# Eight attention units at the front of a fused attention and MLP kernel: two units per 128 partitions, and the maximum subtracted by matrix product

## The chip, the core and the metric

The kernel runs on one core of a Trainium2 chip. The metric is the device time of one execution, in microseconds (us); the median of three runs before the change is 599.78 us (599.56 to 600.16).

The engines named here: TensorE (PE in the profile, PEld for its weight loads) does matrix products into PSUM, VectorE (DVE) and ScalarE (ACT) do elementwise work and read PSUM, GpSimd (POOL) works on SBUF only, SyncE (SP) issues the DMAs.

## The reference

Chunked attention with memory keys, then an MLP with a learned leak. All data are float32.

```python
batch, n_heads, seq, head_dim = 4, 8, 768, 64;  n_mem = 8
chunk, left_ctx, right_ctx = 32, 16, 8
for c in range(seq // chunk):            # 24 chunks of 32 queries
    k_ctx = k[:, :, max(0, 32*c - 16) : min(seq, 32*c + 40)]
    k_full, v_full = concat(mem_k, k_ctx), concat(mem_v, v_ctx)   # up to 64 keys
    scores = q_c @ k_full.T / 8
    a = exp(scores - max(scores));  a = a / (sum(a) + 1e-9)
    out[:, :, chunk c] = a @ v_full
x = out, heads side by side              # 3072 x 512
h = x @ w_in                             # 512 x 2048
g = max(h, 0) + alpha * min(h, 0)
return g @ w_out                         # 2048 x 512
```

## The kernel before, in words

**Units.** Attention is cut into 32 units: a half sequence of 384 tokens (BT) of one batch, times a pair of heads. Four units (NPAIR) make one block of x with 384 tokens and 512 features. Unit u fills feature slice k = u % 4 of half u // 4. The first eight units (NWIN) form blocks 0 and 1. They go another way than the later 24, and the change is about this way; it is written in `windows(u)`.

**One front unit**, step by step, all float32:

- `load_first(u)`: two DMAs into one of four buffers `early` (NSET): queries and keys (656 KB), then values (256 KB). In the queries the two heads stand block-diagonally, with zeros, so that one product serves both heads.
- `score_products(u)` (L300): two filler products (`stir`, L298; eight for unit 0), then 12 products with 128 rows (both heads), 64 output rows and 64 keys. Each float32 product is two instructions. The result is one PSUM bank, `s0` or `s1` by turns: 128 partitions by 6 windows of 64 keys.
- `top` (VectorE, L505 to L509): hides keys outside the sequence and takes the maximum of each window; `less` (VectorE, L513) subtracts it into SBUF; `exps` (ScalarE, L517); `total` and `inverse` (VectorE, L521 and L524).
- `scale` (GpSimd, L534 and L538, three instructions): multiplies with the inverse and writes into `ew`, where each 64-key window has its place in a zeroed field of 128.
- `turn` (L541): one filler product and six 128 x 128 transposes on TensorE, into banks `o0` and `o1`; `keep` (ScalarE, L551, twice) copies them to SBUF.
- `values` (L553): 8 products with 128 rows, 64 output rows and 96 columns, into bank `o2` or `a` by turns.
- `split` (L465): x is kept as a high part (`xh`, ScalarE, L474) and a low part (`xl`, VectorE, L477), both in the reduced float format that TensorE takes in one pass.

**The MLP.** For each block and each of 16 slices f of the hidden width, `up` (L723) makes 12 products of 384 columns (4 feature slices x 3 combinations of high and low parts), `below`, `bend`, `high` and `low` (L732 to L745) apply the leak and split the result, `down` (L753) makes 9 products of 512 columns. For f below 2 the four feature slices of `up` are steps of their own, so each can start when its own unit's x is there. Blocks 0 and 1 alternate for the first nine slices.

**Weights** are loaded as 64-bit integers' raw halves and rebuilt on the chip (`decode`, L609 to L650): ScalarE rebias (L622), a gather on VectorE or ScalarE (L630), VectorE `ends` (L634) and `join` (L638), ScalarE `high` (L646), VectorE `low` (L649). Two buffers `a` hold the work in progress. The weights 12 to 15 later take the place of the four `early` buffers.

**Order.** Nothing is left to a run-time scheduler. Every piece is a `step(engine, cost, function, reads, writes, rest)`. The planner (`Plan.send`) works out what remains behind each step, adds the entries of SHIFT by step number, and deals steps to each engine's queue, the longest remainder first, among those that its own costs and due times say are ready. Each engine, SP with its DMAs too, then runs its queue strictly in that order.

Of the kernel before, what the change touches and what calls it, by code (L numbers as in the profile page):

```python
# [102 lines left out]
STIR = (8, 2, 1)  # L103
# [4 lines left out]
NWIN, NSET = 2 * NPAIR, 4  # L108

STARTS_WIN = (0, 2 * LEFT, NKT - KW)  # L110
NQ = NT * NJ * 2 * CH
NV = NT * 2 * D

# [6 lines left out]
SHIFT = {3: -3.7, 9: -2.7, 10: 2.2, 11: 5.5, 44: 3.5, 63: -3.2, 65: -3.3, 96: -3.1, 103: -3.8, 112: 8.6, 114: 3.6, 116: -15.4, 174: 3.9}  # L120
# [61 lines left out]
def body(ctx: ExitStack, tc: tile.TileContext, qvw, kw, first, w_in, w_out, alpha, out):  # L182
# [17 lines left out]
    ps_a = ctx.enter_context(tc.tile_pool(name="ps_a", bufs=1, space=bass.MemoryType.PSUM))  # L200

# [19 lines left out]
    for ew in ews:  # L221
        nc.gpsimd.memset(ew, 0.0)
# [6 lines left out]
    state = {}  # L229
# [70 lines left out]
    def score_products(u):  # L300
        blk, pr = divmod(u, NPAIR)
        st = state[u]
        s_ps = ps_s.tile([P, 512], F32, name="s_ps", tag=f"s{u % 2}")
        stir(s_ps, STIR[0] if u == 0 else STIR[1])
        st["s"] = s_ps[:, :2 * NJ * KW].rearrange("p (n k) -> p n k", k=KW)
        t = early[u % NSET]
        q = t[:, :NQ].rearrange("p (c x) -> p c x", c=NT * NJ)
        keys = t[:, NQ:NQ + NT * NKT].rearrange("p (t k) -> p t k", t=NT)
        for n in range(2 * NJ):
            for i in range(2):  # L310
                t, j = n // NJ * 2 + i, n % NJ
                nc.tensor.matmul(  # L312
                    out=st["s"][i * 2 * CH:(i + 1) * 2 * CH, n],
                    lhsT=q[:, t * NJ + j],
                    rhs=keys[:, t, STARTS_WIN[j]:STARTS_WIN[j] + KW],
                    start=True, stop=True,
                )
# [114 lines left out]
    def value_products(u):  # L432
        st = state[u]
        pool, tag, _ = bank(u)
        st["a"] = pool.tile([P, 512], F32, name="a_ps", tag=tag)
# [29 lines left out]
    def split(u, ak="a"):  # L465
# [5 lines left out]
        cols = slice(at_ * BT, (at_ + 1) * BT)  # L471

        def high():
            nc.scalar.copy(out=ring[k][0][:, cols], in_=st["a"][:, :BT])  # L474

        def low():
            nc.vector.tensor_tensor(out=ring[k][1][:, cols], in0=st["a"][:, :BT], in1=ring[k][0][:, cols].bitcast(F32),  # L477
                                    op=ALU.subtract)
# [3 lines left out]
        step(ACT, 0.48, high, reads=[ak], writes=xh)  # L482
        step(DVE, 0.56, low, reads=[ak, xh[0]], writes=xl)

    def load_first(u):
        blk, pr = divmod(u, NPAIR)
        t = early[u % NSET]

        def load(lo, hi):
            nc.sync.dma_start(out=t[:, lo:hi], in_=first[blk, pr, :, lo:hi])  # L490

        state[u] = {}
        step(SP, 1.6, partial(load, 0, NQ + NT * NKT), writes=[("qk", u % NSET)], rest=due(u))
        step(SP, 0.78, partial(load, NQ + NT * NKT, NQ + NT * NKT + NV), writes=[("fv", u % NSET)], rest=due(u))

    def windows(u):

        st = state[u]
        sk, tks, ak = ("s", u % 2), [("o", 0), ("o", 1)], ("o", 2) if u % 2 else "a"
# [11 lines left out]
        def less():  # L511
            st["e"] = es[u % 2][:, :, :KW]
            nc.vector.tensor_tensor(out=st["e"], in0=st["s"], in1=st["mx"].broadcast_to([P, NJ * 2, KW]),  # L513
                                    op=ALU.subtract)

        def exps():
            nc.scalar.activation(out=st["e"], in_=st["e"], func=AF.Exp, scale=SCALE)  # L517
# [440 lines left out]
```

## Time and profile before

| what | value |
|---|---|
| median of the runs | 599.78 us |
| span of the profiled execution | 597.5 us |
| TensorE busy | 591.1 us, 99% |
| VectorE busy | 386.7 us, 65% |
| ScalarE busy | 210.6 us, 35% |
| GpSimd busy | 36.5 us, 6% |
| read from HBM, written | 41.95 MB, 6.29 MB |
| filler products (L298) | 30, of them 22 into the score banks |

The span reaches from the first to the last instruction of one profiled execution; the device time of the runs is some 2.3 us longer than the span. "Busy" for TensorE counts a product until its modelled end, so a filler product counts as busy as well. In the answers quoted below, a row of the chain has its start, its length and what ran; a row of a group has line, engine, operation, output and input, shapes and count, then busy time and mean length in ns, then the engine's idle time before it and what ended that.

### The profile page before, as it was taken

What the parts mean: (1) busy time and instruction counts of PE and PEld (TensorE: products, weight loads), DVE (VectorE), ACT (ScalarE), POOL (GpSimd) and SP (SyncE); (2) the same over time, 40 slices, a digit from 0 to 9 for tenths busy, and PEclk for the clock granted to TensorE, in tenths of its full rate; (3) what the DMA queues carried; (4) which work ended last, traced back from release to release, by engine and by line L of the source; (5) the groups of instructions that cost most, each with busy time, mean ns of one, the idle gap of its engine ahead of it and who ended that gap; (6) DMA issues with size and microseconds to landing.
All of it is one profiled execution on the core that took longest, in us unless ns stands there. A gap on an engine that the chain in (4) does not pass through costs nothing.

```text
span 597.5 us, 10975 instructions
## 1 busy us (share of the span) xinstructions
PE 591.1 (99%) x4430; PEld 505.7 (85%) x4430; DVE 386.7 (65%) x904; ACT 210.6 (35%) x580; POOL 36.5 (6%) x61
## 2 busy tenths in 40 slices
PE   8999999999999999999999999999999999999997
PEld 4789999888998989989898888888888888888885
DVE  5888898887959768685885852861862771530530
ACT  3788888644222504323233302302400411210201
POOL 3510000010001101010010100100100100000000
PEclk9999999999999999999999999999999999999999
DMA  8999500222040302403304003003101000000001
GB/s 337 359 399 407 226 0 1 66 65 89 2 152 2 101 23 79 153 1 100 94 8 150 4 1 100 2 0 109 62 2 36 1 0 36 36 1 0 1 1 71
DMA packets 21076, 48.96 MB, mean 82 GB/s; under 512 B 2464, under 2 KB 5792, under 8 KB 21024
## 3 DMA queue, kind: packets, MB, share of 16 engines
q1 hardware_dynamic: 20880, 48.12, 22.8%
q8 instruction: 35, 0.57, 0.4%
q14 instruction: 17, 0.14, 0.1%
q10 hardware_dynamic: 144, 0.13, 0.1%
HBM read 41.95 MB, written 6.29 MB: 81 GB/s over the span
## 4 chain that ended last, share of the span: by engine, by line
PE 96%; DMA 3%; SPq 0%; ACT 0%; issue 0%; ACTq 0%
PE h_ps L723 45%; PE o_ps L753 44%; PE a_ps L438 3%; DMA early<-first 3%; PE s_ps L337 2%; PE a_ps L559 1%; PE o_ps L546 1%; PE s_ps L312 0%; SPq L490 0%; PE o_ps L298 0%; ACT o_t L810 0%; PE s_ps L298 0%; ACTq L810 0%
## 5 line engine op out<-in xcount | busy, mean ns | idle before, releaser
L723 PE MATMUL h_ps<-xh,w 128*128 128x384 f32 (+1 forms) x896 | 248.8, 358 | 0.0
L723 PEld LDWEIGHTS h_ps<-xh,w 128*128 128x128 f32 x896 | 164.9, 188 | 16.0
L753 PE MATMUL o_ps<-w,gh 128*128 128x512 f32 x528 | 162.7, 389 | 0.0
L723 PE MATMUL h_ps<-xl,w 128*128 128x384 f32 (+1 forms) x448 | 162.6, 363 | 0.0
L732 ACT ACTIVATE g<-h_ps 128x384 f32<-128x384 f32 (+1 forms) x112 | 60.4, 540 | 194.7 <-PE h_ps L723 129.1
L735 DVE SCALAR_TENSOR_TENSOR g<-g,rise,h_ps 128x384 f32<-128x384 f32 (+1 forms) x112 | 74.7, 668 | 74.8 <-ACT g L732 74.1
L753 PEld LDWEIGHTS o_ps<-w,gh 128*128 128x128 f32 x528 | 99.1, 188 | 20.4
L413 DVE STREAM_TRANSPOSE pt<-e 32x64 f32<-32x64 f32 (+1 forms) x336 | 99.4, 301 | 7.4 <-POOL e L392 2.0
L753 PE MATMUL o_ps<-w,gl 128*128 128x512 f32 x264 | 102.8, 389 | 0.0
L723 PEld LDWEIGHTS h_ps<-xl,w 128*128 128x128 f32 x448 | 84.1, 188 | 10.2
L753 PE MATMUL o_ps<-w,xh 128*128 128x512 f32 x240 | 74.8, 393 | 0.0
L753 PEld LDWEIGHTS o_ps<-w,gl 128*128 128x128 f32 x264 | 49.6, 188 | 10.2
L477 DVE TENSOR_TENSOR xl<-a_ps,xh 128x384 fp32r<-128x384 f32 x32 | 17.6, 554 | 61.0 <-ACT xh L474 60.4
L753 PEld LDWEIGHTS o_ps<-w,xh 128*128 128x128 f32 x240 | 45.0, 188 | 8.9
L741 DVE CAST gh<-g 128x512 fp32r<-128x512 f32 (+1 forms) x72 | 28.8, 401 | 30.6 <-PE o_ps L753 28.2
L474 ACT CAST xh<-a_ps 128x384 fp32r<-128x384 f32 x32 | 15.0, 483 | 95.0 <-PE a_ps L438 93.7
L392 POOL TENSOR_TENSOR e<-e,den 128x384 f32<-128x384 f32 x24 | 22.8, 949 | 419.6 <-DVE den L389 270.0
L745 DVE TENSOR_TENSOR gl<-g,gh 128x512 fp32r<-128x512 f32 (+1 forms) x72 | 46.6, 648 | 1.7
L371 ACT ACTIVATE e<-s_ps,mx 128x64 f32<-128x64 f32 x144 | 43.4, 318 | 11.1 <-DVE mx L363 11.1
L753 PE MATMUL o_ps<-w,xl 128*128 128x512 f32 x120 | 46.8, 390 | 0.0
L371 ACT ACTIVATION_READ_ACCUMULATOR e<-s_ps,mx 128x1 f32 x144 | 30.4, 211 | 0.0
L810 ACT COPY o_t<-o_ps 128x512 f32<-128x512 f32 x21 | 12.2, 591 | 44.6 <-PE o_ps L753 44.2
(58 smaller groups left out, 380.2 us busy)
## 6 DMA issues: line engine op xcount, KB each, us to landing
w_t<-w_in SPq DMA_DIRECT2D x16, 512.0 KB, 10.0
w_t<-w_out SPq DMA_DIRECT2D x16, 512.0 KB, 10.1
qk<-kw SPq DMA_DIRECT2D x24, 272.0 KB, 4.3
v_t<-qvw SPq DMA_DIRECT2D x24, 256.0 KB, 2.8
out<-o_t SPq DMA_DIRECT2D x23, 256.0 KB, 2.1
early<-first SPq DMA_DIRECT2D x8, 656.0 KB, 6.2
qk<-qvw SPq DMA_DIRECT2D x24, 192.0 KB, 4.8
early<-first SPq DMA_DIRECT2D x8, 256.0 KB, 6.3
```

What stands on the lines that cost most here:

```text
L371: nc.scalar.activation(out=st["e"][:, i], in_=st["s"][h2][:, n], func=AF.Exp, scale=SCALE, bias=d["mx"][:, u - us[0], n, h2:h2 + 1], accum ...
L392: nc.gpsimd.tensor_tensor(out=st["e"], in0=st["e"], in1=st["den"].broadcast_to([P, NJ * 2, KW]), op=ALU.mult)
L413: nc.vector.transpose(out=pts[u % NPT][quad * CH:(quad + 1) * CH, j, t0:t0 + n1 - n0].rearrange("p t h q -> p (t h) q"), in_=(st["e"], zer ...
L438: nc.tensor.matmul(out=st["a"][h2 * D:(h2 + 1) * D, t * TQ:(t + 1) * TQ], lhsT=st["v"][:, t, h2, :], rhs=pts[u % NPT][:, :, t, h2, :], sta ...
L474: nc.scalar.copy(out=ring[k][0][:, cols], in_=st["a"][:, :BT])
L477: nc.vector.tensor_tensor(out=ring[k][1][:, cols], in0=st["a"][:, :BT], in1=ring[k][0][:, cols].bitcast(F32), op=ALU.subtract)
L723: nc.tensor.matmul(out=h["ps"][:, :n_cols], lhsT=ws[f, 0][:, wk, k * P:(k + 1) * P], rhs=parts(blk, k)[1](xk), start=(k == 0 and n == 0), ...
L732: nc.scalar.activation(out=h["g"], in_=h["ps"][:, :n_cols], func=AF.Relu, scale=-1.0)
L735: nc.vector.scalar_tensor_tensor(out=h["g"], in0=h["g"], scalar=rise[:, f:f + 1], in1=h["ps"][:, :n_cols], op0=ALU.mult, op1=ALU.add)
L741: copy(out=h["gh"], in_=h["g"])
L745: nc.vector.tensor_tensor(out=h["gl"], in0=h["g"], in1=h["gh"].bitcast(F32), op=ALU.subtract)
L753: nc.tensor.matmul(out=o_ps[tt], lhsT=h[gk][:, tt * P:(tt + 1) * P], rhs=ws[f, 1][:, wk], start=(f == first_f and i == 0), stop=(f == last ...
```

## The change

For the eight front units:

- Two units share a load of 928 KB: unit u has its 64 feature rows in half u % 2 of the 128 partitions, the two heads side by side instead of block-diagonal. There are two such buffers. Values are laid out chunk by chunk (64 keys of one chunk on 64 partitions) in four buffers of their own, 768 KB for two units. So NSET is 6, and the buffers are lent from weights 10 to 15.
- Scores are 24 products with 64 rows, 32 output rows and 64 keys. The filler ahead of them goes, except the opening eight of unit 0; the filler ahead of the transposes goes.
- The maximum is subtracted by one product on TensorE that accumulates into the score bank: minus the identity times the maxima, repeated over 64 keys. ScalarE's exponential then reads PSUM.
- GpSimd scales in one instruction, into a dense `ew` with two windows side by side in 128; three transposes do for a unit, into one bank, `o0` or `o1` by turns, and one copy follows.
- Values are 24 products with 64 rows, 64 output rows and 32 columns. Products of the upper and the lower 64 rows write to two banks, which are the former `o2` and `a` as one tile `beside`; every unit uses both. `split` reads the two banks in one instruction and puts the 32-column runs in their order.
- The planner's costs follow, and SHIFT has other entries.

```diff
-STIR = (8, 2, 1)
+STIR = 8
-NWIN, NSET = 2 * NPAIR, 4
+NWIN, NSET = 2 * NPAIR, 6
-SHIFT = {3: -3.7, 9: -2.7, 10: 2.2, 11: 5.5, 44: 3.5, 63: -3.2, 65: -3.3, ...}
+SHIFT = {6: -4.7, 7: -7.8, 8: 5.8, 10: 3.8, 69: 1.0, 102: 8.1, 116: 5.3, 176: 7.4}
...
+    beside = ps_a.tile([P, 2, 512], F32, name="beside")
...
-    early = [wps[NF - NSET + i, 0].tile([P, NQ + NT * NKT + NV], F32, name="early", tag="w") for i in range(NSET)]
-    ews = [turned.tile([P, 2, NJ, P], F32, name=f"ew{i}", tag=f"pt{i}") for i in range(NPT)]
+    early = [wps[NF - NSET + i, 0].tile([P, NQ + NKEY if i < 2 else 2 * NVW], F32, name="early", tag="w") for i in range(NSET)]
+    ews = [turned.tile([P, NJ * 2, KW], F32, name=f"ew{i}", tag=f"pt{i}") for i in range(NPT)]
...
-        stir(s_ps, STIR[0] if u == 0 else STIR[1])
+        if u == 0:
+            stir(s_ps, STIR)
+        rows = slice(u % 2 * D, (u % 2 + 1) * D)
+        both = early[u // 2 % 2][rows]
...
         for n in range(2 * NJ):
             for i in range(2):
+                t, j = divmod(i * 2 * NJ + n, NJ)
+                for h2 in range(2):
+                    at_ = (2 * i + h2) * CH
+                    nc.tensor.matmul(
+                        out=st["s"][at_:at_ + CH, n],
+                        lhsT=q[:, h2, t * NJ + j],
+                        rhs=keys[:, h2, t, STARTS_WIN[j]:STARTS_WIN[j] + KW],
+                        start=n == 0, stop=True, skip_group_check=True,
+                    )
...
-        step(SP, 1.6, partial(load, 0, NQ + NT * NKT), writes=[("qk", u % NSET)], rest=due(u))
-        step(SP, 0.78, partial(load, NQ + NT * NKT, NQ + NT * NKT + NV), writes=[("fv", u % NSET)], rest=due(u))
+        step(SP, 2.32, load, writes=[("qk", two % 2)], rest=due(2 * two))        # load_first(two)
+        step(SP, 1.95, load, writes=[("fv", two)], rest=due(2 * two))            # load_first_v(two)
...
         def less():
-            nc.vector.tensor_tensor(out=st["e"], in0=st["s"], in1=st["mx"].broadcast_to([P, NJ * 2, KW]),
-                                    op=ALU.subtract)
+            nc.tensor.matmul(out=st["s"], lhsT=minus, rhs=st["mx"].broadcast_to([P, NJ * 2, KW]),
+                             start=False, stop=True, skip_group_check=True)
         def exps():
-            nc.scalar.activation(out=st["e"], in_=st["e"], func=AF.Exp, scale=SCALE)
+            nc.scalar.activation(out=st["e"], in_=st["s"], func=AF.Exp, scale=SCALE)
...
+            for m in range(NJ):
+                nc.tensor.transpose(st["t"][:, m * P:(m + 1) * P], ew[:, m * P:(m + 1) * P], eye)
...
+            for x in range(2 * NJ):
+                for r in range(2):
+                    rows = slice(r * KW, (r + 1) * KW)
+                    for h2 in range(2):
+                        nc.tensor.matmul(
+                            out=st["a"][h2 * D:(h2 + 1) * D, r, x],
+                            lhsT=v[rows, x, h2],
+                            rhs=et[rows, x % NJ, x // NJ, h2],
+                            start=True, stop=True,
+                        )
...
-        step(PE, 1.2, partial(score_products, u), reads=[("qk", u % NSET)], writes=[sk], rest=due(u))
+        step(PE, 0.75, partial(score_products, u), reads=[("qk", u // 2 % 2)], writes=[sk], rest=due(u))
         step(DVE, 0.66, top, writes=[sk, ("mx", u % 3)])
-        step(DVE, 0.55, less, reads=[sk, ("mx", u % 3)], writes=e_keys(u))
-        step(ACT, 0.52, exps, writes=e_keys(u))
+        step(PE, 0.78, less, reads=[("mx", u % 3)], writes=[sk], rest=due(u))
+        step(ACT, 0.53, exps, reads=[sk], writes=e_keys(u))
...
-        step(PE, 0.85, values, reads=[("q", u % NKB), ("fv", u % NSET)], writes=[ak], rest=due(u, 1))
+        step(PE, 0.65, values, reads=[("q", u % NKB), ("fv", u // 2)], writes=ak, rest=due(u, 1))
```

More of the change, by code (lines that the diff above doesn't have):

```diff
@@ L181, in body @@
 @with_exitstack
-def body(ctx: ExitStack, tc: tile.TileContext, qvw, kw, first, w_in, w_out, alpha, out):
+def body(ctx: ExitStack, tc: tile.TileContext, qvw, kw, first, firstv, w_in, w_out, alpha, out):
     nc = tc.nc
@@ L228, in body @@
     step = plan.add
-    state = {}
+    state = {u: {} for u in range(NWIN)}
     NU = NHALF * NPAIR
```

146 lines of the change are left out of this document (64 added, 82 removed).

## The prediction

> **What bounds the kernel now.** I read the page first, then the chain of waits in order of time, then busy times by stretch.
>
> ```profile
> span 597.5 us, 10975 instructions
> PE 591.1 (99%) x4430; PEld 505.7 (85%) x4430; DVE 386.7 (65%) x904; ACT 210.6 (35%) x580; POOL 36.5 (6%) x61
> DMA  8999500222040302403304003003101000000001
> ```
>
> TensorE is busy for 99% of the span; the DMA engines are full only in the first four or five slices (15 us each). The chain (start, length, what) shows from when TensorE alone decides:
>
> ```profile
> 9.84 9.18 DMA early<-first
> ...
> 19.06 0.88 PE a_ps L559 x16
> 19.94 0.32 PE o_ps L298
> 20.26 0.66 PE o_ps L546 x6
> 20.92 0.81 PE a_ps L559 x16
> 21.73 0.54 PE s_ps L298 x2
> 22.27 0.85 PE s_ps L312 x24
> ...
> 42.25 2.08 PE o_ps L753 x9
> 44.33 2.10 PE h_ps L723 x12
> ```
>
> From 19.06 on every link is a TensorE product, almost to the end. L298 is filler: constant products nobody reads. I call S the moment 44.33, when the up-products of weight 2 begin. Before it TensorE must finish all eight front units (scores L312, transposes L546, values L559), four groups of up-products and two of down-products. Busy times on either side (first row all; the last row the filler alone):
>
> ```profile
> 4.87:44.33 39.46, 38.30 (x458) 30.28 (x458) 32.29 (x73) 27.52 (x53) 11.62 (x27) 1.00 1.01 383
> 44.33:593.79 549.46, 549.37 (x3967) 474.41 (x3965) 353.91 (x830) 181.06 (x526) 22.77 (x24) 1.00 0.17 59
> 4.87:44.33 39.46, 7.40 (x23) 1.72 (x22) 1.00 1.01 383
> ```
>
> The columns are length, TensorE, weight loads, VectorE, ScalarE, GpSimd, clock, DMA share, GB/s. After S TensorE idles 0.1 us in 549. So the change can pay only by moving S, and what S moves, the end moves. Of the 39.46 us before S, the work is 8 x (0.85 + 0.66 + 0.81) + 4 x 2.10 + 2 x 2.08 = 31.1 us; 8.3 are filler (7.4 busy) and idle (1.2).
>
> **The change, part by part.**
>
> *Loads.* Front scores begin as loads land:
>
> ```profile
> 1.46 3.48 PE L298 MATMUL s_ps<-busy 128*128 128x512 bf16 x8 [1.46 <-DVE warm L224]
> 4.87 0.92 PE L312 MATMUL s_ps<-early 128*64 128x64 f32 x24
> 6.38 0.92 PE L312 MATMUL s_ps<-early 128*64 128x64 f32 x24
> 8.03 0.92 PE L312 MATMUL s_ps<-early 128*64 128x64 f32 x24 [0.19 <-DMA early<-first]
> 9.69 0.92 PE L312 MATMUL s_ps<-early 128*64 128x64 f32 x24
> ```
>
> One 656 KB load lands every 1.65 us, 398 KB/us. The new pair load has 928 KB: the first lands 0.68 us later, at 5.55, but serves two units; the second at 7.9. Reading the planner's rule (longest remaining path first, plus SHIFT), I put w_in 0 third (lands 9.2), then values of pair 0 (11.1), queries and keys of pair 2 (13.4), values 1 (15.4), pair 3 (17.7), w_in 1, values 2 (20.9), w_out 0, values 3 (24.1). SP holds pair 2's load until unit 1's scores are done (about 7.2); behind it wait the later loads, but the transfers queued already last until 11.1. The front needs 6784 KB instead of 7296, in 8 DMAs instead of 16, so 1.3 us of transfer goes. Cost on the path: 0.7 us at the start.
>
> *TensorE products of a unit.* Nearest rows (busy us, mean ns):
>
> ```profile
> L312 PE MATMUL s_ps<-early 128*64 128x64 f32 x192 | 7.3, 226 | 0.3 <-DMA early<-first 0.2
> L559 PE MATMUL a_ps<-qk,early 128*64 128x96 f32 x128 | 7.0, 252 | 0.4 <-DMA early<-first 0.4
> L546 PE MATMUL o_ps<-eye,ew 128*128 128x128 f32 x48 | 6.5, 273 | 0.0
> L337 PE MATMUL s_ps<-qk 64*32 64x64 f32 x1152 | 14.9, 224 | 0.0
> ```
>
> Per instruction: L312 38 ns with two tiles of the array at work, 64 columns; L559 55 ns, two tiles, 96 columns; L337 12.9 ns, eight tiles, 64 columns. A tile is thus held 76 ns for 64 columns and 109 for 96, so 43 for 32.
> - Scores: 48 instructions of L337's shape, but a unit's lie in one half of the rows, so four tiles: 76/4 = 19 ns, 0.91 us. Ends: 0.62 (L337's price) and 1.82 (L312's 38 ns). I take 0.85, nearer L337, whose shape it is.
> - Values: 48 instructions of 32 columns on four tiles: 43/4 = 11 ns, below anything shown, so 12.9: 0.62 us; the far end is 1.82 again.
> - The subtraction: two instructions of 384 columns on the whole array. Three of L546's 136 ns twice is 0.82; by the chain's 0.66/6 = 110 ns, 0.66. I take 0.70. That the moving operand repeats one element 64 times no row shows; ends 0.66 and 0.82.
> - Transposes: three for six, 0.33 to 0.41; I take 0.37.
> - Filler: 22 of 30 go; the eight opening ones stay, ahead of 4.94.
>
> Sum 2.54 us a unit, 20.3 for eight, against 18.6 before without filler: the useful work grows by 1.7 us, as the subtraction comes to TensorE. The gain can only be the 8.3 us of filler and idle.
>
> The Trainium skill, "TensorE: Matmul & The Clock Gate", in its section "Wait — 56ns, not 53.3ns?", says that the distance between matmul starts never falls below about 25 ns, however few the columns. By that the 96 small instructions of a unit would take 2.4 us, not 1.47, an estimate from the page's figure that puts 7.4 us on the sum. L337's 12.9 ns disagrees, and the measurement decides.
>
> *The other engines.*
>
> ```profile
> L509 DVE TENSOR_REDUCE mx<-s_ps 128x6 f32<-128x384 f32 x8 | 4.5, 558 | 0.3
> L517 ACT ACTIVATE e<-e 128x384 f32<-128x384 f32 x8 | 4.4, 544 | 7.1 <-DVE e L513 7.1
> L521 DVE TENSOR_REDUCE den<-e 128x6 f32<-128x390 f32 x8 | 4.3, 542 | 0.0
> L513 DVE TENSOR_TENSOR e<-s_ps,mx 128x384 f32<-128x384 f32 x8 | 4.4, 546 | 0.9 <-POOL ew L538 0.9
> L551 ACT COPY qk<-o_ps 128x384 f32<-128x384 f32 x16 | 7.2, 495 | 2.6 <-PE o_ps L546 2.4
> L392 POOL TENSOR_TENSOR e<-e,den 128x384 f32<-128x384 f32 x24 | 22.8, 949 | 419.6 <-DVE den L389 270.0 <-ACT e L371 87.4 <-ACT g L732 58.7
> L534 POOL TENSOR_TENSOR ew<-e,den 128x256 f32<-128x256 f32 x8 | 5.3, 660 | 17.2 <-DVE den L524 9.1 <-DVE s_ps L505 6.5 <-ACT a L622 1.6
> 42.35 1.22 DVE L649 TENSOR_TENSOR w<-a,w 128x1024 fp32r<-128x1024 f32 x1
> ...
> 52.32 1.22 DVE L649 TENSOR_TENSOR w<-a,w 128x1024 fp32r<-128x1024 f32 x1
> 54.75 4.18 PE h_ps L723 x24
> ```
>
> VectorE loses the eight subtractions (4.4 us), ScalarE eight of sixteen copies (3.6), GpSimd goes from three instructions a unit to one of 0.95; its two start-up instructions for the minus matrix take the place of two clears, all ahead of the first landing. None of it is on the chain, yet VectorE and ScalarE carry the weight decode, which is the second bound: weight 2 is finished at 42.35 + 1.22 = 43.57, 0.76 us ahead of S, and weight 3 at 53.54 for a use at 54.75. With ScalarE lighter by 3.6 us and VectorE by more, weight 2 comes at about 40.0, if their waits stay as long. The strided views of the split may cost up to its own length again (0.5 us a unit) on engines that idle 7 and 12 us before S; I take nothing, the price of plain rows.
>
> *New waits.* Both engines now meet TensorE once more in each softmax, behind whatever products stand ahead; other units' products fill that. And every unit's outputs use the same two banks, so values of the next unit wait for the split of this one. One round, before, at its quickest and its slowest:
>
> ```profile
> 29.90 0.88 PE L559 MATMUL a_ps<-qk,early 128*64 128x96 f32 x16
> 30.83 0.48 ACT L474 CAST xh<-a_ps 128x384 fp32r<-128x384 f32 x1 [0.23 <-PE a_ps L559]
> 31.34 0.56 DVE L477 TENSOR_TENSOR xl<-a_ps,xh 128x384 fp32r<-128x384 f32 x1 [0.48 <-ACT xh L474]
> ...
> 15.48 0.83 PE L559 MATMUL a_ps<-qk,early 128*64 128x96 f32 x16
> 16.60 0.48 ACT L474 CAST xh<-a_ps 128x384 fp32r<-128x384 f32 x1
> 18.37 0.54 DVE L477 TENSOR_TENSOR xl<-a_ps,xh 128x384 fp32r<-128x384 f32 x1
> ```
>
> That is 2.0 to 3.4 us. The first values can start at about 12.4: scores to 6.4, maximum to 7.1, subtraction behind unit 1's scores to 7.9, exponential to 8.5, sum and inverse to 9.3, scaling to 10.3, transposes behind other subtractions to 11.4, copy to 12.0, a hop; their data are there from 11.1. So the last split ends between 28 and 40. Two single up-products (2.10/4 each), four bend operations of some half a microsecond and a down-product of 2.08 follow: about 5 us. At 2.6 us a round that is 12.4 + 20.8 + 5 = 38.2, just hidden.
>
> The six buffers now lent to the front belong to weights 10 to 15, not 12 to 15; these land long ahead of their use: the transfers end in the fifth slice, when TensorE is at weight 5. That costs nothing unless TensorE caught up with them.
>
> **The sum.** First landing 5.55 + units 20.3 + MLP products 12.6 = 38.4 without any wait. For waits I take 2.0: the idle 1.2 of before, 0.4 for the landing at 13.4, 0.4 for the added hop. S = 40.4 against 44.33: 3.9 us sooner, a little behind the decode's 40.0, so the two bounds agree. The profiled span becomes 593.6. The span of before lies 2.3 us below its median of 599.78, which I add: 595.9.
>
> **Rivals.**
> - *Dense front.* Waits near zero and decode sooner, since w_in 0 lands at 9 instead of 16: S = 38.4, 593.9; with the cheap ends of the products 593. Against it: VectorE is busy for 82% and ScalarE for 70% of that stretch, and each takes its work strictly in a written order.
> - *Late x or decode.* Rounds of 3.2 us on the one pair of banks give 12.4 + 25.6 + 5 = 43.0, that is 598.5. For it: ScalarE and VectorE took 3.4 us for one round in this trace; against it: they lose 8 us of work before S.
> - *Small products do not overlap in one half of the rows; slower.* If scores cost L312's price, 1.82 instead of 0.85, S = 40.4 + 7.8 = 48.2 and the time 603.7. It decides from a mean of about 20.5 ns for the 96 instructions of a unit (I take 15.3): (44.33 - 5.55 - 12.6 - 2.0)/8 leaves 3.02 us a unit, less 1.07 for subtraction and transposes. For it: no row has four tiles of one half. Against: L312 itself already overlaps two tiles that share all rows. The Trainium skill, same page, "Part 3: Packing small matmuls — row/col tiling", speaks for this rival: a weight load runs beside a matmul only if their row groups differ, which here they never do.
> - *The clock falls without filler.* The opening eight took 3.48 us, 435 ns each, against 270 each for the pair at 21.73; products of the first four units (10 us) slowed in that ratio add 6.1 us: 602.0. Against: by my schedule no gap reaches a microsecond. The same page ("What's actually happening") lets the clock fall only after an idle window of about 3.4 us; the row of 435 ns agrees with its slow start, and no run here shows a fall.
>
> **How the numbers follow.** Forecast 0.51 (594.3 to 597.6), dense 0.10, late 0.21, no overlap 0.11, clock 0.07. About 0.2% (1.2 us) is what a measurement of this kernel can tell from no change. Faster: 0.51 + 0.10 + two thirds of late = 0.75; same: the rest of late and some of the clock's = 0.10; slower 0.15. The range runs from the dense case, 593.3, to the upper end of late, 599.8; above it lie the slow cases.
>
> **What would show it.** Right: first scores near 5.5; TensorE idle of 1 to 3 us between there and S; S at 39 to 42; 1.2 to 1.6 us for 96 small products; subtraction 0.65 to 0.8 a unit; clock 1.00; nothing idle after S. Wrong: rounds of the shared banks above 3 us with up-products waiting on x; waits of the first up- or down-products for a weight; 64-row products above 20 ns each; or idle that turns up between 45 and 65 us, where the decode of weight 3 has 1.2 us to spare.

## The result: slower, and the profile after

The changed kernel takes 610.18 us (median, 609.92 to 611.7) against 599.71 us for the kernel before on the same chip: ratio 1.018, 95% interval 1.0165 to 1.0194. The forecast was 595.9 us and a faster kernel; the time is 14.3 us above it, and the change makes the kernel slower.

From the page of the changed kernel, the span, the engines' busy times and the transfers of instructions:

```profile
span 608.5 us, 11771 instructions
PE 598.4 (98%) x4848; PEld 510.8 (84%) x4848; DVE 383.5 (63%) x896; ACT 209.0 (34%) x572; POOL 32.9 (5%) x45
q8 instruction: 38, 0.62, 0.4%
```

The same columns as in the prediction (length, TensorE, weight loads, VectorE, ScalarE, GpSimd, clock, DMA share, GB/s), for the two stretches before and behind S, then for slices of 5 us:

```profile
5.37:54.00 48.63, 45.10 (x875) 35.37 (x876) 29.35 (x66) 25.68 (x45) 8.95 (x11) 0.82 1.02 405
54.00:604.00 550.00, 549.28 (x3966) 474.35 (x3965) 353.67 (x830) 181.25 (x525) 22.72 (x24) 1.00 0.15 50
...
15.00:20.00 5.00, 1.61 (x88) 1.38 (x87) 2.12 (x7) 1.12 (x2) 1.95 (x2) 1.00 0.99 403
20.00:25.00 5.00, 4.97 (x98) 3.66 (x102) 2.06 (x5) 1.45 (x3) 0.00 (x0) 0.51 1.00 404
25.00:30.00 5.00, 5.00 (x101) 3.36 (x97) 2.20 (x7) 2.03 (x4) 0.82 (x1) 0.50 1.03 413
...
35.00:40.00 5.00, 5.00 (x92) 4.05 (x95) 3.00 (x8) 3.86 (x7) 1.09 (x1) 0.79 1.03 407
```

Two of these slices in the kernel before:

```profile
15.00:20.00 5.00, 4.58 (x90) 3.63 (x85) 4.44 (x14) 2.65 (x6) 2.01 (x6) 1.00 1.03 405
20.00:25.00 5.00, 5.00 (x73) 3.78 (x73) 3.96 (x10) 4.68 (x10) 2.57 (x6) 1.00 1.06 352
```

S, the start of the up-products of weight 2, is 54.00 instead of 44.33. Almost all of the loss is ahead of it. The slices show two things that the kernel before does not have: from 15 to 20 TensorE works for 1.61 us of 5, and from 20 to 37 its clock is half while it is busy for every microsecond.

The chain of waits (start, length, what) names the first and gives the price of the second:

```profile
15.10 0.80 PE s_ps L327 x48
15.90 0.71 PE beside L568 x39
16.61 3.42 issue
20.03 0.52 PE beside L568 x9
20.55 1.43 PE s_ps L327 x48
...
27.80 1.58 PE s_ps L532 x2
29.38 1.44 PE beside L568 x48
...
37.67 0.48 PE o_ps L554 x3
38.15 0.65 PE s_ps L532 x2
...
39.64 0.83 PE beside L568 x48
...
54.00 2.10 PE h_ps L730 x12
```

L327 are the scores, L532 the subtraction, L554 the transposes, L568 the values, L730 the up-products. The 3.42 us lie in the midst of one group of value products, after 39 of 48. Only the first of the 48 waits for a semaphore (the signal by which an engine or a load releases another), so no engine and no load of data held TensorE there. "issue" is time for which the profile shows no releaser. At full clock a unit takes 0.80 + 0.65 + 0.48 + 0.83 = 2.76 us; at half clock the same groups take 1.43, 1.58 and 1.44.

The first groups, from the timeline, are slow as well. From 10.25 on the scores of two units take 1.53 us, ahead of that 2.40. The trace's clock record of this run begins with full clock at 9.83; for the time ahead of it the clock column of the slices prints 1.00, so the durations decide there:

```profile
5.37 2.40 PE L327 MATMUL s_ps<-early 64*32 64x64 f32 x96 [0.32 <-DMA early<-first]
7.79 2.54 PE L532 MATMUL s_ps<-mx,minus 128*128 128x384 f32 x4
10.25 1.53 PE L327 MATMUL s_ps<-early 64*32 64x64 f32 x96
```

The loss adds up. At full clock the work from 5.37 to S would be 8 x 2.76 + 12.6 = 34.7 us. To it come 3.5 us idle (48.63 less 45.10), 17.07 / 2 = 8.5 for the half clock from 20.07 to 37.13, and 4.46 / 2 = 2.2 for the slow start up to 9.83, if the clock was half all that time. That is 48.9 against 48.63 measured.

### The profile page after: what moved, and what is told of

Its sections match the earlier page's. It is cut to its first block, busy times and chain, and to the rows that moved or that the text cites. A ratio compares the mean times of both kernels' runs of the same rounds, so it can differ in the third digit from the quotient of the medians.

```text
span 608.5 us, 11771 instructions
## 1 busy us (share of the span) xinstructions
PE 598.4 (98%) x4848; PEld 510.8 (84%) x4848; DVE 383.5 (63%) x896; ACT 209.0 (34%) x572; POOL 32.9 (5%) x45
## 4 chain that ended last, share of the span: by engine, by line
PE 97%; DMA 1%; issue 1%; ACT 0%; POOL 0%; DVE 0%; ACTq 0%; DVEq 0%; POOLq 0%
PE h_ps L730 44%; PE o_ps L760 25%; PE beside L760 18%; PE s_ps L352 2%; PE a_ps L453 2%; PE beside L568 1%; PE s_ps L532 1%; PE s_ps L327 1%; PE beside L453 1%; PE o_ps L554 1%; DMA early<-first 1%; ACT o_t L817 0%; POOL ew L547 0%; DVE den L541 0%; ACT e L537 0%
## 5 line engine op out<-in xcount | busy, mean ns | idle before, releaser
L730 PE MATMUL h_ps<-xh,w 128*128 128x384 f32 (+1 forms) x896 | 249.5, 359 | 0.0
L730 PEld LDWEIGHTS h_ps<-xh,w 128*128 128x128 f32 x896 | 165.4, 188 | 16.0
L730 PE MATMUL h_ps<-xl,w 128*128 128x384 f32 (+1 forms) x448 | 163.1, 364 | 0.0
L730 PEld LDWEIGHTS h_ps<-xl,w 128*128 128x128 f32 x448 | 84.4, 188 | 9.9
L760 PE MATMUL o_ps<-w,gh 128*128 128x512 f32 x288 | 88.8, 390 | 0.0
L760 PE MATMUL beside<-w,gh 128*128 128x512 f32 x240 | 73.9, 389 | 0.0
L760 PEld LDWEIGHTS o_ps<-w,gh 128*128 128x128 f32 x288 | 54.1, 188 | 11.0
L760 PE MATMUL o_ps<-w,gl 128*128 128x512 f32 x144 | 56.1, 390 | 0.0
L760 PEld LDWEIGHTS beside<-w,gh 128*128 128x128 f32 x240 | 45.1, 188 | 9.4
L760 PE MATMUL o_ps<-w,xh 128*128 128x512 f32 x160 | 50.0, 394 | 0.0
L760 PE MATMUL beside<-w,gl 128*128 128x512 f32 x120 | 46.8, 390 | 0.7 <-ACT o_t L817 0.7
L495 DVE TENSOR_TENSOR xl<-a_ps,xh 128x384 fp32r<-128x384 f32 x16 | 8.9, 557 | 54.6 <-ACT xh L492 54.1
L760 PEld LDWEIGHTS o_ps<-w,xh 128*128 128x128 f32 x160 | 30.0, 187 | 5.5
L760 PEld LDWEIGHTS o_ps<-w,gl 128*128 128x128 f32 x144 | 27.0, 188 | 5.5
```

The costliest lines, as they stand in the source:

```text
L495: nc.vector.tensor_tensor(out=xs[1], in0=st["a"], in1=xs[2], op=ALU.subtract)
L730: nc.tensor.matmul(out=h["ps"][:, :n_cols], lhsT=ws[f, 0][:, wk, k * P:(k + 1) * P], rhs=parts(blk, k)[1](xk), start=(k == 0 and n == 0), ...
L760: nc.tensor.matmul(out=o_ps[tt], lhsT=h[gk][:, tt * P:(tt + 1) * P], rhs=ws[f, 1][:, wk], start=(f == first_f and i == 0), stop=(f == last ...
```

## The experiments

Theory: TensorE runs out of instructions (a unit now has 202 products and weight loads, 98 before), and the stop and the low activity of small products halve the clock. Rivals: the missing filler alone; the width of the products themselves; another cause in the order of the work. Each run was timed in rounds beside the kernel before; ratios are to that. S is always the start of the up-products of weight 2 in the profiled execution.

### The filler taken from the kernel before (e1_before_nofill)

```diff
-STIR = (8, 2, 1)
+STIR = (8, 0, 0)
```

> The kernel before, with all filler but the opening eight products taken out; nothing else moves. Instruction-supply theory (TensorE outran the fetch of its instructions, which stood behind a full set of DMA transfers; the 3.4 us stop let the clock fall): the front units keep 92 TensorE instructions each, so no stop above 2 us, the clock stays at 1.00, and at least the 1.9 us of filler on the chain go: 595 to 598.5. Filler theory (it was the missing filler alone that let the clock fall): half clock for at least one stretch of 3.4 us in the first 40 us, 601 or more.

Measured: 599.02 us, ratio 0.9988 (0.9979 to 0.9997), S 43.96. TensorE's longest waits (in all, times, longest), then one slice:

```profile
PE s_ps L312 <- DMA early<-first: 2.1, 2, 1.3
PE s_ps L312 <- DVE mx L509: 1.5, 2, 0.8
```

```profile
15.00:20.00 5.00, 3.36 (x48) 2.73 (x46) 3.87 (x11) 2.63 (x6) 2.16 (x6) 0.82 1.03 407
```

7.4 us of filler gone bring 0.7 us (0.12%): what it filled are waits for loads and for the maxima, and the clock falls for 3.4 us. The time lies between the ranges of the two theories. Missing filler alone doesn't make the kernel slower, and none of these waits is named issue.

### Filler put back into the changed kernel (e2_after_fill)

```diff
-        if u == 0:
-            stir(s_ps, STIR)
+        stir(s_ps, STIR if u == 0 else 2)
...
+            stir(st["t"], 1)
```

> The changed kernel with the filler of before put back: two constant products ahead of each unit's scores, one ahead of its transposes. Supply theory: the fetch still comes late, the stop shrinks to 1.5 to 3 us because filler slows the use of instructions, and the big filler products bring the clock back within one or two stretches of 3.4 us instead of five: 601 to 606. Filler theory: no stop and a clock of 1.00, at most 600.

Measured: 610.01 us, ratio 1.0171 (1.0156 to 1.0186), S 54.27. TensorE's longest wait, then the filler's share of the stretch up to S:

```profile
PE s_ps L326 <- issue: 3.4, 3, 1.6
```

```profile
5.40:54.27 48.87, 6.21 (x15) 2.02 (x22) 0.97 0.99 388
```

The time is above the range of either theory. The clock record of this run begins at 13.16 (the 0.97 counts full clock ahead of that, but there the scores of one unit took 1.50 us, as at half clock), and behind that it shows half clock for 3.41 us instead of 17.07. The filler costs 6.2 us itself. Two long stops stay, 1.6 and 1.5 us, and both begin at full clock, at 25.10 and 31.02. So much of the clock can be bought, at the price of what it saves, and the stops are not a consequence of a low clock.

### The same work in fewer, wider products (e3_after_wide)

```diff
-        for n in range(2 * NJ):
+        for n in range(0, 2 * NJ, 2):
...
-                        out=st["s"][at_:at_ + CH, n],
+                        out=s_ps[at_:at_ + CH, n * KW:(n + 2) * KW],
-                        rhs=keys[:, h2, t, STARTS_WIN[j]:STARTS_WIN[j] + KW],
+                        rhs=keys[:, h2, t, :2 * KW],
...
-            for x in range(2 * NJ):
+            for x in range(0, 2 * NJ, NJ):
-                            out=st["a"][h2 * D:(h2 + 1) * D, r, x],
+                            out=st["a"][h2 * D:(h2 + 1) * D, r, x:x + NJ],
-                            rhs=et[rows, x % NJ, x // NJ, h2],
+                            rhs=et[rows, :, x // NJ, h2],
```

> The changed kernel with the same columns streamed in fewer instructions: scores as 12 products of 128 columns instead of 24 of 64, values as 8 of 96 instead of 24 of 32, on the same tiles of the array (the windows' pairing of queries, keys and values is given up, so this leaves part of the computation wrong and stands for its time only). TensorE instructions per unit go from 202 to 90. Supply theory: no stop of TensorE around 16 us, no fall of the clock after 10 us, 595 to 598. Rival (stop or clock come from the small row-half products or the missing filler, whatever their number): stop or half clock stay, 604 or more.

Measured: 596.39 us, ratio 0.9945 (0.993 to 0.9959), S 40.23. TensorE's longest wait, then the stretch up to S:

```profile
PE s_ps L327 <- DMA early<-first: 1.8, 2, 1.2
```

```profile
5.30:40.23 34.93, 32.61 (x427) 24.13 (x428) 28.82 (x66) 25.07 (x45) 9.02 (x11) 1.00 1.02 411
```

The run gives up the windows' pairing, so it stands for its time only. With everything else of the change in place, and 90 instructions a unit instead of 202, stop and half clock are gone and S is where the prediction had it. This separates the change's plan from its instructions, but number and width of the products changed together.

### Many small instructions in the kernel before (e4_before_many)

```diff
-        for _ in range(num):
-            nc.tensor.matmul(out=t, lhsT=busy[:, :P], rhs=busy, start=True, stop=True)
+        many, cols = {STIR[0]: (num, DM), STIR[1]: (40, 26), STIR[2]: (16, 32)}[num]
+        m = P if many == num else CH
+        for _ in range(many):
+            nc.tensor.matmul(out=t[:m, :cols], lhsT=busy[:, :m], rhs=busy[:, :cols], start=True, stop=True)
```

> The kernel before with its filler (but the opening eight) cut into many small products: 40 of 26 columns ahead of scores, 16 of 32 ahead of transposes, in 32 output rows. TensorE instructions per unit go from 98 to 204, columns stay about the same. Supply theory: one or more stops of TensorE of 1 to 4 us within the first 35 us with no releaser shown, and a clock at half after them: 602 to 612. Rival (number of instructions does not matter): at most the 0.5 us a unit that the smaller products last longer, 599.5 to 603, with no stop and a clock of 1.00.

Measured: 606.99 us, ratio 1.0122 (1.0105 to 1.0139), S 51.94. TensorE's waits, then the filler's own time from 6 us to S:

```profile
PE s_ps L314 <- issue: 0.7, 1, 0.7
PE s_ps L300 <- issue: 0.5, 1, 0.5
```

```profile
6.00:51.94 45.94, 12.83 (x408) 11.21 (x408) 1.00 0.90 337
```

The same number of instructions does bring stops that the kernel before doesn't have, but short ones, and the clock of the profiled execution never fell. The cut filler took some 13 us instead of 7.4, which is most of the loss. So the run shows that number makes stops, and leaves their size open.

### The early loads cut into pieces (e5_after_split)

```diff
+    def pieces(out, src, n):
+        w = out.shape[-1] // n
+        for i in range(n):
+            nc.sync.dma_start(out=out[:, i * w:(i + 1) * w], in_=src[:, i * w:(i + 1) * w])
...
-            nc.sync.dma_start(out=early[two % 2], in_=first[two])
+            pieces(early[two % 2], first[two], 4)
...
-            nc.sync.dma_start(out=early[2 + two], in_=firstv[two])
+            pieces(early[2 + two], firstv[two], 4)
...
+            pieces(raw[k][:, j].rearrange("p m b -> p (m b)"), srcs[i][f], 2 if f < 5 else 1)
```

> The changed kernel with each front load issued as four DMAs of a quarter of its columns, and the weights 0 to 4 as two halves; the same bytes in the same order. Packet theory (a fetch of TensorE's instructions waits until the DMA engines have finished the transfer they are in, one sixteenth of 928 KB lasting 2.3 us, so pieces of a quarter let it through sooner): the stop around 16 us goes or stays under 0.7 us, the clock does not fall after 10 us, S at 41 to 43, 596.5 to 599.5. Rival (the fetch waits for all that stands in the queues, whatever the size of a transfer, or the stop is no matter of DMA): a stop of 2.5 to 4 us and half clock after it, 607 to 612.

Measured: 605.66 us, ratio 1.0099 (1.0072 to 1.0126), S 51.60. The stop, then a slice at half clock:

```profile
PE beside L573 <- issue: 1.3, 1, 1.3
```

```profile
25.00:30.00 5.00, 5.00 (x70) 2.67 (x59) 2.69 (x7) 0.97 (x2) 0.21 (x2) 0.50 0.93 297
```

Only the size of other transfers was changed, and the stop went from 3.42 to 1.3 us. What TensorE lacks there comes through the DMA engines. The rest of the expectation failed: the stop did not shrink below 0.7 us, the clock fell all the same, from 20.87 to 34.53, and S is 51.60 instead of 41 to 43. The Trainium skill, "DMA: Bandwidth & Descriptors", section "Queues, rings and completion order", says that each DMA engine takes turns between its queues a packet at a time. Smaller pieces ahead of the instructions (the trace records rows of 1856 and 1536 bytes for the front loads instead of 7424 and 6144) shorten the stop, which agrees; how rows make up a packet no run here shows.

### Better openings, and two tiles for the outputs (e6_split_open10, e7_split_open10_two, e8_after_open10)

e6 is e5 with ten opening filler products; e8 is the changed kernel with ten and nothing else (`STIR = 10`). e7 is e6 with `o2` and `a` as two tiles again, each split on its own.

> As the kernel with split loads, and with ten opening filler products instead of eight, so that TensorE has work from 1.5 us until the first scores' data are there. Theory: full clock by about 6.5 us instead of 9.8, the first two units' products 1 to 2 us sooner done, 595 to 598, that is 0.5 to 1.5 below the kernel with split loads alone. Rival (the clock's start is a matter of the moment, not of the gap ahead of the first scores): within 0.4 us of it.

> As the one before, with the two output banks as two tiles again and the split of a front unit as two instructions of 192 columns on each engine. Theory: the last block's products into the fourth bank no longer wait for ScalarE's copy of the third (0.7 us idle and some 0.4 more at the end of the changed kernel), while the eight more instructions on ScalarE and VectorE stay hidden: 0.8 to 1.3 us below the one before. Rival: the longer split holds back the next unit's values and takes 0.3 to 1 us more than it gives.

> The changed kernel with ten opening filler products instead of eight and nothing else. Supply theory: a warm start only brings TensorE to the missing instructions sooner, the stop begins about 1.5 us earlier and is about as much longer, the clock falls again, 608.5 to 611. Rival (the cold start, not the stop, is the main loss): 606 or less.

Measured: e6 607.92 us, ratio 1.0109 (1.0071 to 1.0147), S 51.78; e7 605.71 us, ratio 1.0082 (1.0056 to 1.0109), S 51.14; e8 608.75 us, ratio 1.0153 (1.0136 to 1.017), S 50.94. The clock record begins with full clock at 5.9 to 6.7 in these three, at 9.83 in the changed kernel. But e3 and e14, which open with eight products like the changed kernel, have it from 4.20 and 4.33, e5 from 10.63, and e10 below, with ten, from 41.60. So the number of opening products doesn't settle when full clock comes, and neither theory on the opening is shown. The clock also differs between the runs of one kernel: one of e7's took 600.91 us at a mean clock of 0.996, another 607.98 at 0.985. e7's profiled span, 604.3, lies 553.2 us behind S, as before the change (597.5 - 44.33); the changed kernel's lies 554.5 behind. So the shared tile cost 1.3 us behind S; its row is shown further down. (e6, with the shared tile, has 554.4.) In e8 the clock was half for one stretch only, but there were more stops:

```profile
PE s_ps L327 <- issue: 3.1, 2, 2.5
PE beside L568 <- issue: 2.7, 1, 2.7
```

### Smaller pieces still, and a filler product between (e9_split8_open10_two, e10_split8_fill1)

```diff
-            pieces(early[two % 2], first[two], 4)
+            pieces(early[two % 2], first[two], (1, 2, 8, 8)[two])
...
-            pieces(early[2 + two], firstv[two], 4)
+            pieces(early[2 + two], firstv[two], 8)
...
-            pieces(raw[k][:, j].rearrange("p m b -> p (m b)"), srcs[i][f], 2 if f < 5 else 1)
+            pieces(raw[k][:, j].rearrange("p m b -> p (m b)"), srcs[i][f], 4 if f < 5 else 1)
```

e9's edit is against e7; e10 is e9 with one more:

```diff
-        if u == 0:
-            stir(s_ps, STIR)
+        stir(s_ps, STIR if u == 0 else 1)
```

> As the kernel with split loads, ten opening products and two output tiles, but the second pair's queries and keys in 2 pieces, the later ones and all values in 8, the weights 0 to 4 in 4. Packet theory: the fetch comes sooner still, no stop of TensorE above 0.5 us ahead of S (1.1 us with quarters). If the clock falls only after a stop of over about 1 us: clock 1.00, S 41 to 44, 596 to 599. Rival (small products alone count too little for the clock, stop or no stop): no stop, but half clock again from about 20 us, 602 to 606.

> As the one before, with one filler product of 512 columns ahead of each unit's scores. If stops and too little activity were the two losses of the change, both are now mended: clock 1.00 from about 6 us, no stop above 0.5 us, S 42.5 to 44.5, 597 to 599.3. Rival (another loss, so far hidden by these two): S of 46 or more with the clock at 1.00.

Measured: e9 612.26 us, ratio 1.0192 (1.0166 to 1.0217), S 58.39; e10 612.82 us, ratio 1.0214 (1.0197 to 1.0231), S 59.24. Both miss. One slice of e9 shows why: DMA share and rate fell, because the many short loads are issued one by one, 0.43 us each (a link of its chain stands below it), and TensorE waits for data instead.

```profile
15.00:20.00 5.00, 2.43 (x80) 2.02 (x84) 0.64 (x3) 0.04 (x1) 0.07 (x1) 0.86 0.72 192
```

```profile
23.93 0.43 SPq L508
```

e10 answers another question. Two slices, then two links of its chain, value products both:

```profile
20.00:30.00 10.00, 10.00 (x195) 6.72 (x193) 4.68 (x14) 3.12 (x8) 1.93 (x2) 1.00 0.75 205
30.00:40.00 10.00, 10.00 (x175) 6.47 (x172) 4.02 (x14) 3.12 (x8) 1.66 (x2) 1.00 0.73 206
```

```profile
34.76 1.44 PE a_ps L576 x48
...
42.09 0.83 PE a_ps L576 x48
```

TensorE was busy without a gap in these 20 us, yet at 34.76 the 48 products took 1.44 us, as at half clock, and 0.83 only behind the clock record's first entry, at 41.60. (Ahead of that entry the clock column has nothing to go by and prints 1.00; the durations decide.) In this run small products thus kept TensorE busy without lifting its clock, and with no stop ahead of them above 0.5 us.

### Gains for the kernel before (e11_before_late_nofill, e12_before_less_on_pe)

e11 leaves the filler out of the later units only; e12 leaves all of it out but the opening and moves the subtraction to TensorE, the order untouched.

```diff
-        stir(s_ps, STIR[0] if u == 0 else STIR[1])
+        stir(s_ps, STIR[0] if u == 0 else STIR[1] if u < 6 else 0)
...
-            stir(st["t"][0], STIR[2])
+            stir(st["t"][0], STIR[2] if u < 3 else 0)
```

And e12's:

```diff
-            nc.vector.tensor_tensor(out=st["e"], in0=st["s"], in1=st["mx"].broadcast_to([P, NJ * 2, KW]),
-                                    op=ALU.subtract)
+            nc.tensor.matmul(out=st["s"], lhsT=minus, rhs=st["mx"].broadcast_to([P, NJ * 2, KW]),
+                             start=False, stop=True, skip_group_check=True)
```

> The kernel before without the filler ahead of the scores of units 6 and 7 and ahead of the transposes of units 3 to 7, where the chain is TensorE alone. If TensorE alone bounds there: 1.3 to 1.9 us sooner, 597.9 to 598.5. If the decode stands right behind (weight 2 finished 0.76 us ahead of its use): 0.5 to 0.8 us, 598.9 to 599.3.

> The kernel before with one part of the change alone: the maximum subtracted by a product on TensorE, and no filler but the opening eight. Loads, scores, transposes and values stay as before, 96 TensorE instructions a unit. My sum: 5.2 us of new products for 8.3 us of filler and idle, VectorE 4.4 us lighter: S 42.5 to 44, no stop, clock 1.00 or one stretch of half: 597.5 to 599.5. Rival (the added hop through TensorE's queue delays every softmax): S above 45, over 600.5.

Measured: e11 598.63 us, ratio 0.9976 (0.9967 to 0.9986), S 43.82; e12 606.78 us, ratio 1.0112 (1.0097 to 1.0127). e11 is 0.24% faster than the kernel before, and the fastest here that does all of the work: little, since loads and waits stand right behind the filler. In e12 TensorE waits for one maximum: VectorE's order has a step of the weight decode ahead of it, which itself waits 2.6 us for ScalarE. The clock then falls for 6.8 us.

```profile
PE s_ps L516 <- DVE mx L513: 3.3, 1, 3.3
```

The time is in the rival's range, over 600.5 us. The subtraction on TensorE needs an order made for it; what it would bring to the kernel before, with such an order, this run leaves open.

### Both losses mended at once (e13_both_mended)

```diff
-STIR = 10
+STIR = 12
...
-        if u == 0:
-            stir(s_ps, STIR)
+        stir(s_ps, STIR if u == 0 else 2 if u > 1 else 0)
```

The lines are against e7.

> The changed kernel with its first loads in four column pieces (weights 0 to 4 in halves), two separate output tiles, twelve opening filler products, and two filler products ahead of the scores of units 2 to 7. Theory (the loss is the stop of TensorE for want of instructions and the half clock after it, and nothing else): the filler of full columns and rows holds the clock, so granted clock 1.00 from about 7 us on, stops of 1.2 us or less in all, S 43 to 46, of which about 4 us is the filler itself; 598 to 600.5 us. Rival (there is a further loss beside these two): clock 1.00 and short stops but S of 47 or more, over 601 us. Second rival (two filler products don't hold the clock between so many small ones): a stretch of 0.50, S 48 to 52, 602 to 606 us.

Measured: 603.72 us, ratio 1.007 (1.0055 to 1.0085), S 49.90. TensorE's waits named issue, the stretch up to S, and the filler's share of it:

```profile
PE a_ps L576 <- issue: 1.6, 1, 1.6
...
PE s_ps L323 <- issue: 0.4, 1, 0.4
```

```profile
6.34:49.90 43.56, 39.64 (x881) 30.66 (x888) 29.59 (x74) 25.78 (x53) 8.95 (x11) 0.96 0.99 352
```

```profile
6.34:49.90 43.56, 2.55 (x6) 1.11 (x12) 0.96 0.99 352
```

Neither loss was fully mended, so this is no clean test: stops of 2.0 us, more than the theory allowed, and half clock for one stretch of 3.4, as in the second rival. The expectation's first rival, S of 47 or more from a third cause, has the number right but not the reason: work 34.7, idle 43.56 - 39.64 = 3.9, filler 2.6 (some of its products aren't recorded), clock 3.4 / 2 = 1.7 give 42.9 of 43.56. Less than a microsecond is left to any other cause. Two of the four runs had a mean clock of 1.00 and still took 603.3 and 603.6 us.

### Fewer products for the values only (e14_values_wide)

The values part of e3's edit alone.

> The changed kernel with the values of a front unit as 8 products of 96 columns in place of 24 of 32 (part of the products' results is thereby another one), scores unchanged: 138 products and weight loads a unit, between 90 (no stop) and 202 (a stop of 3.4 us). Supply theory: TensorE's instructions last longer, the stop shrinks to 0.5 to 2 us or comes later; the clock may still fall, since the scores stay small; S 43 to 50, 599 to 606 us. Rival (the number of instructions doesn't matter, the stop has another cause in the order of the work): a stop of 3 to 4 us near 16.6 as in the changed kernel, S 51 or more, over 607 us.

Measured: 604.34 us, ratio 1.0082 (1.0053 to 1.0111), S 46.93. Its chain has the stop:

```profile
17.73 2.46 issue
```

Like e3 it gives up a pairing and stands for its time only. Its clock fell too, for 10.24 us from 21.40. There is no stop at 90 instructions a unit, one of 2.5 us at 138, one of 3.4 at 202. So the number matters, though the stop is longer than the 2 us that the supply theory allowed. The next reading says why.

### Where the stops fall

A count of products and weight loads from the program's start to each stop, as stretches that end there. First the changed kernel, then e8, whose four stops are all listed:

```profile
0.00:16.61 16.61, 14.73 (x349) 9.07 (x349) 7.95 (x23) 6.10 (x11) 3.98 (x13) 1.00 0.90 346
```

```profile
0.00:16.10 16.10, 13.84 (x349) 8.18 (x349) 8.14 (x23) 6.14 (x11) 3.99 (x13) 1.00 0.88 345
0.00:24.40 24.40, 19.40 (x476) 12.07 (x476) 11.14 (x30) 8.32 (x16) 4.81 (x14) 0.93 0.93 367
0.00:28.91 28.91, 23.34 (x603) 14.65 (x604) 14.36 (x38) 10.57 (x20) 5.78 (x16) 0.94 0.94 375
0.00:37.48 37.48, 29.39 (x730) 19.65 (x731) 18.45 (x49) 15.07 (x29) 8.01 (x18) 0.95 0.96 382
```

and e14, which has other products, and the loads cut in e5:

```profile
0.00:17.73 17.73, 14.31 (x348) 8.61 (x349) 10.16 (x28) 7.25 (x14) 4.79 (x14) 1.00 0.91 365
```

```profile
0.00:17.67 17.67, 15.62 (x348) 9.51 (x349) 8.18 (x23) 6.12 (x11) 3.99 (x13) 1.00 0.90 308
```

Whatever runs there and whenever it is, the stop comes after 349 weight loads, or 476, 603 or 730: steps of 127. The long stops of the other runs fall there too, or 222, within three loads; e4, with other instructions between, stopped after 224 and 352. (One wait named issue is not of this kind: e9's of 2.4 us at 13.80, after 264 loads, ahead of scores whose loads were just landing. Its cause stays open.) The page agrees: 4848 products in 38 transfers of the queue q8 instruction are 128 a transfer, and 0.62 MB / 38 is 16 KB. So instructions come in pieces of 127 products with their loads, and a stop is a piece that comes late.

The trace records each transfer of that queue, and these times show it directly (us; "goes on" is the first product behind load 349):

| run | front loads | load 222 starts | transfer | stops | goes on |
|---|---|---|---|---|---|
| changed kernel | whole | 13.24 | 17.61 to 18.57 | 16.61 | 20.03 |
| e8 | whole | 12.28 | 16.48 to 17.44 | 16.10 | 18.85 |
| e14 | whole | 12.29 | 17.68 to 18.71 | 17.73 | 20.18 |
| e5 | quarters | 14.07 | 16.47 to 17.59 | 17.67 | 18.96 |
| e10 | up to eight pieces | 18.13 | 19.08 to 20.02 | no stop | |
| before | whole | 18.30 | 21.42 to 22.46 | no stop | |

In the first four rows TensorE goes on 1.4 to 1.5 us behind the end of a transfer (1.2 to 1.7 in the other stops), whatever the length of the stop. Beside whole loads the transfer begins 3.1 to 5.4 us behind load 222, beside quarters 2.4, beside the smallest pieces 1.0. So it is the wait behind the loads that makes a piece late. What makes the queue ask for a piece, the traces don't show.

Whether a late piece stops TensorE follows from how long the piece before lasts: from load 222 to load 349 it is 10.6 us in the kernel before (18.30 to 28.92), 3.4 to the stop in the changed one and 5.4 in e14. The border itself was passed 6.8 us after the one before in the changed kernel (20.03 - 13.24) and 7.9 in e14 (17.73 + 2.46 - 12.29). A piece that lasts 10.6 us hides such a delay; pieces of 3.4 and 5.4 don't.

## Why the prediction was wrong

**Right.** First scores at 5.37, foreseen near 5.5. VectorE, ScalarE and GpSimd were no bound in this run, and the shared pair of output banks held up nothing ahead of S: TensorE's only long wait there was the stop. The subtraction took 0.65 us, foreseen 0.70. The break-even condition for small products was met: 96 of a unit took 0.80 + 0.83 = 1.63 us, 17 ns each against 20.5 needed. Without the losses S would be where it was put: 5.37 + 34.7 is 40.1 against the 40.4 forecast; e3, with fewer and wider products but 2.3 us idle, had 40.23. That the two agree so closely is luck, as the terms below show.

**The step that failed is the sum's silence on how TensorE gets its instructions.** The unit's 202 products and loads for 98 were counted for their durations only. Nothing in the sum, and no rival, had a term for fetching them, although the page of before lists the transfers on an instruction queue and its DMA engines were full in these very microseconds:

```profile
q8 instruction: 35, 0.57, 0.4%
```

That is 3.4 us for the stop itself; what followed was dearer.

**The clock rival had the right sign and the wrong size.** It was given 0.07 and 6.1 us, argued away with "by my schedule no gap reaches a microsecond". A gap did, for the reason above: the 3.41 us ahead of the fall at 20.07 hold 3.38 us of the stop. In all twelve falls that these traces record ahead of S, TensorE idled for 0.85 us (e6) or more of the 3.41 us ahead; yet e8 passed its 2.5 us stop at 28.91 without a fall, so a gap is not enough. The clock cost 8.5 + 2.2 = 10.7 us, of which the 2.2 of the start are a matter of the moment: e3 and e14 open alike and had full clock from 4.20 and 4.33. The 435 ns of the opening filler in the profile of before said that TensorE starts slow; that it stays slow when small products follow was not weighed. The Trainium skill, "TensorE: Matmul & The Clock Gate", section "What's actually happening", has full clock return after one busy window of about 3.4 us. Here it took 17 us of unbroken work in the changed kernel and over 20 in e10: the measurement decides, and busy time alone is not what counts. What brings the clock back stays open, a product's share of the array among the candidates: in e8 one stretch of 3.4 us was enough, with the same products.

**Terms that were mis-sized.** Values 0.83 instead of 0.62, transposes 0.48 instead of 0.37, scores 0.80 instead of 0.85, subtraction 0.65 instead of 0.70: 2.76 a unit instead of 2.54, so 1.8 us in all. The 12.9 ns taken for 32-column products on four tiles was the price of eight; they cost 17 ns, as the 64-column ones do. The 2.0 us of waits don't show in the changed kernel, where a slow TensorE left the other engines time, and that about makes up for it; e3 idled 2.3 us. The remark that a unit's row groups never differ holds for the scores only: the values' products alternate between the two halves of the rows, and at 17 ns both cost the same.

**"Nothing idle after S" was wrong.** One group of down-products at the end shows the price of the shared tile, from the page of the changed kernel:

```profile
L760 PE MATMUL beside<-w,gl 128*128 128x512 f32 x120 | 46.8, 390 | 0.7 <-ACT o_t L817 0.7
```

Products for bank `a` wait there for the copy out of `o2`, because both are one tile now. With the rest of the tail it is the 1.3 us that e7 gave back.

**The gain was small where it could be had.** Most of the 8.3 us of filler and idle covered other waits. Taking out all but the opening gave 0.12% in e1: waits for loads (2.1 us), waits for VectorE (2.1) and half clock (3.41 / 2 = 1.7) came in its place. e11's choice gave 0.24%.

## What to carry to other kernels

Count the instructions of a stage, not only their time: where a stage of short products runs beside full DMA queues, ask how long one piece of instructions lasts and how long the next takes to come. Products that use a small part of TensorE's array count as busy in the profile but may not bring its clock up; read durations against a known full-speed row. And when filler is taken out, first see what it covers.

## What the runs showed of the hardware

TensorE's instructions were fetched while the program ran, 16 KB at a time. A transfer of 16 KB took about 1 us, and TensorE went on 1.2 to 1.7 us behind its end; beside loads of 768 and 928 KB it began so late that TensorE passed the next border only 6.8 to 7.9 us after the last. The clock record changed only in steps of 3.41 us (17.07 us of half clock are five of them), and in e10 products kept the durations of half clock through stretches in which TensorE was busy for 10.00 us of 10. Cutting loads into short pieces helped down to quarters and then hurt, as issuing takes 0.43 us each: the rate fell from about 405 to 192 GB/s.
